# All eight PSUM banks by a table, a leftover load moved to GpSimd, a split last block and a new searched order for a fused linear-attention and MoE kernel

## Chip, cores and metric

One core of one Trainium2 chip. The metric is device time in microseconds (us) for one execution. Most executions of the kernel before agree within about 0.3%. The TensorE clock that the throttle granted is listed for each run as a mean share (1.0 is full clock).

## The reference, cut to what matters

```python
# q, k, v: (8 batches, 8 heads, 576, 64); omega: (128, 64)
def phi(x):                                   # random features, x already scaled
    h = x @ omega.T - (x*x).sum(-1, keepdims=True) / 2
    return exp(h - h.max(-1, keepdims=True)) / sqrt(128)
kv  = einsum('bhsm,bhsd->bhmd', phi(k), v);  z = phi(k).sum(axis=2)
att = einsum('bhsm,bhmd->bhsd', phi(q), kv) / (einsum('bhsm,bhm->bhs', phi(q), z)[..., None] + 1e-6)
x   = att.transpose(0, 2, 1, 3).reshape(4608, 512)
h   = x @ w_in                                # 512 -> 2048, "stage 1"
out = (h * sigmoid(1.702 * h)) @ w_out        # 2048 -> 512, "stage 2"
```

The 576 positions of a head are 512 plus a leftover of 64. The leftovers of all heads form their own small tiles (QL, TL, QKL, VPL) and at the end the ninth row block of the MoE part.

## The kernel before

The program first builds a graph of 1533 operations (1540 after the change). Five fixed lists (`ORDER`) say in which order each engine runs its operations, and a table (`BANK`) says which of the eight PSUM banks (H0 H1 O0 O1 P0 P1 S0 S1) each group of matmuls takes. Waits between engines follow from the graph: an operation waits for what it reads, for a buffer to be free, for the user before it of the same group of matmuls in PSUM, and for the last user of its bank.

```python
def schedule(self):
    self.order = {e: [ops[i] for i in ORDER[e]] for e in ENGINES}
    names = iter(BANK)
    for op in ops:
        for gr in op.opens:
            gr.bank = next(names)
    for op in self.order[PE]:                 # a bank is taken over only after its last user
        for gr in op.opens:
            for o in last.get(gr.bank, ()):
                op.deps.setdefault(o.i, False)
...
# leftover q/k of batch b: by GpSimd with a cast (b >= QL_SW = 2), or f32 by SyncE plus a cast instruction
pool = b >= QL_SW
...
# DMA transposes on SyncE: queries/keys of a tile (TT), leftovers (TL), attention output (XT)
g.add(SP, lambda e: e.dma_start_transpose(tout, tin), ...,
      reads=[("q", s, t), ("k", s, t)], writes=[("Tk", tt), ("Tq", tt), ("tgo", b, t)], ...)
g.add(SP, lambda e: e.dma_start_transpose(xo, xi), ...,
      reads=[("o", os_, 0), ("o", os_, 1)], writes=[("xt", t, b), ("xt", t, b + 1)], ...)
...
attend(0)
for b in range(1, B):
    stage1(b - 1)                             # reads ("xt", t, b - 1)
    if b >= 2:
        stage2(b - 2)
    attend(b)
    if b + 1 < B:                             # loads of the next batch, all on GpSimd
        gate = [("wout", 2)] if b == 1 else [("tgo", b, 2)]
        load_qk(b + 1, 0, 4, ..., after=gate); load_qk(b + 1, 4, 4, ..., after=gate)
        load_ql(b + 1, ..., after=gate);       load_v(b + 1, 0, NT, ..., after=gate)
```

The `gate` says what a load has to wait for beside its own buffer: here that tile 2 of batch b has been transposed.

Names in the profiles: HT, OB, PB and SB are the banks H, O, P and S; XT is the transposed attention output OO, TT and TL are the transposed q/k of a tile and of the leftovers (loaded into QK, and into QL, through QLF where a cast follows); VP and VPL are products with v on GpSimd; TH and GT are the gate of the MoE part on ScalarE and VectorE, OS an output block.

Of the kernel before, what the change touches and what calls it, by code (L numbers as in the profile page):

```python
# [7 lines left out]
ALU = mybir.AluOpType  # L8
# [6 lines left out]
PE = "pe"  # L15
# [3 lines left out]
SP = "sp"  # L19
# [10 lines left out]
BANKS = dict(b0="H0 H1 O0 O1 P0 P1 S0 S1", b1="O1 P0 P1 S0 S1", b2="O1 P0 P1 S0 S1", bv="H0 H1 P0 P1 S0 S1", H="H0 H1", O="O0 O1", Oend="O0 O1 P0 P1")  # L30
# [5 lines left out]
QL_SW = 2  # L36
# [13 lines left out]
    om=(30.0, 0.0, 400.0), qk=(45.0, 1200.0, 770.0), ql=(26.5, 600.0, 630.0), qlc=(26.5, 800.0, 770.0), vl=(26.0, 600.0, 640.0),  # L50
    v=(51.0, 1600.0, 700.0), vw=(51.0, 1200.0, 640.0), qkl=(45.0, 1000.0, 770.0), w=(78.0, 2000.0, 810.0), T=(25.3, 100.0, 1250.0), os=(90.0, 100.0, 620.0),
# [6 lines left out]
        88, 50, 10, 54, 52, 66, 57, 56, 90, 71, 65, 72, 93, 99, 92, 115, 120, 98, 119, 142, 78, 144, 147, 117,  # L58
        152, 80, 146, 153, 125, 105, 83, 126, 132, 110, 107, 86, 219, 134, 137, 159, 113, 221, 253, 164, 140,
        161, 251, 223, 217, 167, 231, 172, 277, 169, 255, 175, 275, 301, 299, 178, 241, 303, 246, 184, 243,  # L60
        181, 265, 249, 187, 267, 270, 193, 279, 273, 196, 202, 313, 383, 211, 315, 289, 318, 205, 291, 294,
        190, 389, 297, 214, 199, 390, 208, 321, 391, 338, 335, 392, 347, 356, 384, 341, 395, 396, 353, 344,
        397, 398, 365, 457, 401, 402, 362, 350, 417, 385, 371, 359, 409, 403, 404, 477, 380, 368, 427, 386,
        437, 377, 467, 432, 429, 556, 472, 487, 374, 469, 447, 492, 562, 489, 449, 563, 557, 452, 564, 558,
        559, 565, 610, 574, 575, 576, 577, 650, 514, 582, 511, 568, 508, 520, 630, 569, 529, 517, 570, 590,
        538, 526, 571, 620, 535, 523, 729, 622, 532, 625, 660, 640, 544, 600, 541, 665, 645, 662, 735, 553,
        605, 602, 730, 642, 547, 550, 736, 763, 737, 731, 732, 755, 687, 738, 684, 693, 741, 681, 783, 742,
        773, 743, 775, 702, 778, 696, 744, 803, 747, 748, 749, 750, 823, 690, 813, 705, 793, 818, 815, 699,
        795, 902, 708, 798, 833, 714, 838, 903, 835, 711, 723, 908, 720, 956, 717, 904, 909, 936, 726, 854,
        910, 860, 905, 863, 857, 928, 914, 866, 911, 869, 915, 946, 920, 966, 875, 971, 948, 916, 917, 976,  # L70
        921, 878, 951, 968, 872, 996, 922, 986, 881, 923, 1129, 890, 884, 991, 1075, 1006, 988, 1101, 899,
        1076, 1011, 1109, 893, 1008, 887, 1081, 1082, 896, 1169, 1083, 1077, 1084, 1078, 1093, 1149, 1094,
        1033, 1119, 1095, 1030, 1027, 1124, 1087, 1042, 1088, 1051, 1036, 1121, 1089, 1139, 1045, 1060, 1090,
        1282, 1039, 1096, 1141, 1144, 1048, 1159, 1274, 1054, 1302, 1248, 1057, 1179, 1161, 1063, 1292, 1164,
        1066, 1181, 1184, 1294, 1249, 1072, 1069, 1322, 1260, 1297, 1250, 1261, 1342, 1251, 1203, 1206, 1266,
        1332, 1267, 1352, 1215, 1212, 1334, 1312, 1262, 1337, 1357, 1263, 1224, 1354, 1221, 1254, 1233, 1314,
        1200, 1255, 1317, 1209, 1218, 1256, 1227, 1257, 1236, 1242, 1427, 1245, 1364, 1428, 1373, 1230, 1268,
        1382, 1239, 1429, 1361, 1269, 1370, 1391, 1415, 1379, 1400, 1416, 1388, 1417, 1397, 1406, 1418, 1367,
        1409, 1410, 1487, 1411, 1376, 1481, 1385, 1394, 1412, 1403, 1482, 1421, 1483, 1433, 1436, 1422, 1442,
        1484, 1445, 1423, 1454, 1451, 1424, 1460, 1488, 1489, 1463, 1439, 1490, 1448, 1430, 1457, 1512, 1505,  # L80
        1466, 1499, 1500, 1501, 1469, 1502, 1526, 1478, 1527, 1506, 1493, 1507, 1475, 1513, 1472, 1494, 1495,
        1514, 1508, 1515, 1496, 1519, 1520, 1521, 1522, 1528, 1529,
    ],
    ACT: [
        51, 89, 9, 60, 61, 59, 70, 73, 75, 74, 101, 68, 102, 95, 100, 97, 122, 124, 129, 154, 151, 156, 127,
        155, 128, 133, 149, 220, 87, 160, 114, 141, 226, 218, 225, 236, 237, 235, 227, 173, 238, 233, 170, 260,
        261, 257, 176, 259, 179, 242, 262, 308, 309, 185, 305, 182, 266, 250, 307, 188, 310, 194, 285, 284,
        197, 286, 203, 283, 281, 212, 206, 191, 215, 200, 209, 339, 336, 393, 348, 357, 342, 345, 354, 399,
        366, 463, 459, 461, 462, 363, 351, 422, 464, 419, 423, 421, 360, 424, 412, 413, 411, 372, 405, 482,
        483, 381, 481, 484, 369, 479, 387, 442, 443, 441, 439, 444, 378, 375, 560, 616, 615, 566, 617, 612,  # L90
        614, 578, 655, 656, 652, 515, 512, 584, 585, 654, 509, 521, 586, 636, 657, 632, 530, 635, 518, 595,
        634, 539, 597, 527, 637, 592, 572, 536, 524, 596, 594, 533, 545, 542, 554, 548, 551, 768, 769, 765,
        733, 688, 770, 759, 757, 685, 758, 767, 739, 694, 788, 682, 787, 789, 790, 703, 785, 697, 808, 745,
        805, 809, 807, 810, 751, 829, 828, 691, 825, 827, 706, 830, 700, 709, 715, 712, 724, 721, 961, 958,
        962, 960, 718, 941, 727, 963, 938, 943, 855, 861, 940, 942, 906, 864, 858, 932, 930, 912, 931, 870,
        867, 876, 918, 982, 981, 983, 980, 978, 879, 873, 1001, 1002, 998, 1000, 1003, 882, 924, 1135, 1133,
        891, 1134, 1131, 885, 1104, 1103, 1136, 900, 1105, 1115, 1114, 894, 1111, 1113, 888, 897, 1173, 1174,
        1171, 1116, 1085, 1175, 1176, 1155, 1153, 1151, 1034, 1079, 1031, 1028, 1043, 1154, 1156, 1052, 1037,
        1046, 1061, 1091, 1288, 1287, 1040, 1284, 1097, 1286, 1049, 1277, 1278, 1289, 1055, 1308, 1276, 1304,
        1058, 1307, 1306, 1064, 1067, 1073, 1070, 1328, 1327, 1326, 1324, 1309, 1348, 1252, 1329, 1344, 1347,  # L100
        1349, 1204, 1346, 1207, 1216, 1213, 1264, 1225, 1222, 1234, 1201, 1210, 1219, 1228, 1258, 1237, 1243,
        1246, 1365, 1374, 1231, 1383, 1240, 1362, 1270, 1371, 1392, 1380, 1401, 1389, 1398, 1419, 1407, 1368,
        1377, 1386, 1395, 1413, 1404, 1434, 1437, 1443, 1485, 1446, 1455, 1452, 1425, 1461, 1464, 1440, 1491,
        1431, 1449, 1458, 1467, 1470, 1479, 1503, 1476, 1473, 1509, 1516, 1497, 1523, 1530,
    ],
    DVE: [
        4, 5, 8, 19, 14, 2, 11, 3, 12, 6, 55, 53, 58, 69, 91, 13, 67, 96, 116, 94, 121, 143, 123, 79, 145, 150,
        118, 148, 81, 106, 84, 85, 82, 108, 111, 109, 112, 138, 135, 139, 136, 222, 254, 165, 162, 163, 252,
        166, 224, 168, 234, 232, 278, 174, 256, 258, 171, 276, 302, 300, 177, 180, 304, 247, 248, 244, 245,
        186, 306, 183, 268, 269, 271, 272, 189, 195, 280, 282, 198, 314, 204, 274, 290, 213, 316, 317, 292,  # L110
        295, 296, 293, 207, 319, 192, 320, 216, 298, 201, 322, 210, 340, 337, 349, 358, 343, 346, 355, 460,
        458, 367, 364, 418, 352, 420, 410, 361, 373, 480, 478, 382, 428, 370, 440, 438, 468, 430, 433, 431,
        473, 474, 488, 434, 448, 470, 493, 471, 490, 450, 451, 376, 379, 453, 491, 454, 494, 613, 611, 651,
        653, 583, 516, 513, 510, 631, 522, 633, 531, 519, 591, 593, 540, 528, 621, 537, 525, 623, 626, 627,
        534, 661, 624, 641, 546, 601, 666, 646, 663, 647, 667, 664, 606, 543, 555, 643, 644, 607, 603, 604,
        552, 764, 549, 756, 766, 689, 686, 695, 786, 774, 683, 776, 784, 779, 777, 780, 704, 804, 698, 806,
        826, 824, 814, 692, 794, 819, 820, 707, 816, 817, 796, 797, 701, 799, 800, 834, 710, 716, 836, 839,
        840, 837, 713, 725, 957, 959, 722, 719, 939, 937, 728, 856, 862, 865, 859, 929, 871, 868, 947, 967,
        949, 972, 950, 973, 877, 979, 977, 952, 953, 969, 970, 874, 997, 999, 987, 880, 883, 1132, 1130, 992,
# [225 lines left out]
def bass_performer_favor__then__act_gelu_quick_kernel(  # L345
# [136 lines left out]

    def load_ql(b, key, ckey, after=()):
        s = b % 2
        pool = b >= QL_SW
        if b in LWB:
            for nm, t, c in (("k", kd, 1), ("q", qd, 0)):
                dst = bass.AP((QL if pool else QLF)[s], 256 * c, [[512, 128], [1, 256]])
# [620 lines left out]
```

## Time and profile before

| | before |
|---|---|
| median of the runs beside the first runs of the change | 324.53 us (324.12 to 325.43, 4 runs) |
| span in the profile | 321.7 us |
| first matmul starts / last matmul ends | 5.67 / 317.71 us |
| first reduction on VectorE (maxima of a projection) | 10.58 us |
| first stage-1 matmul / first GT on VectorE | 26.50 / 28.74 us |
| TensorE time lost in gaps before 40 us / after | 8.3 / 4.7 us |

The gaps are taken from the starts of all matmuls: what each is above the usual distance for its kind. The prediction shows the lines and says how they are read. From 40 us on TensorE is the bound, and it stands still nearly nowhere.

### The profile page before, as it was taken

How to read it: one execution, taken by the hardware profiler on the slowest of the kernel's cores; microseconds unless marked ns; L12 is line 12 of the kernel's file. 1: busy time of each engine (PE TensorE's matmuls, PEld its weight loads, DVE VectorE, ACT ScalarE, POOL GpSimd, SP SyncE). 2: the span in 40 equal slices, each digit the busy share in tenths (PEclk: the TensorE clock that was granted, in tenths of full speed). 3: DMA queues.
4: the chain of work that ended last, by engine and by line, in shares of the span. 5: the costliest groups of instructions: out<-in, count | busy, mean ns of one | idle time of the engine just before them, and what ended most of it. 6: DMA issues, size and time to landing. Idle time of an engine off the chain costs nothing.

```text
span 321.7 us, 5787 instructions
## 1 busy us (share of the span) xinstructions
PE 307.4 (96%) x2246; PEld 151.2 (47%) x2246; DVE 190.7 (59%) x401; ACT 187.3 (58%) x378; POOL 113.1 (35%) x185
## 2 busy tenths in 40 slices
PE   1798999999999999999999999999999999999994
PEld 1574554445544544454454544454544444444442
DVE  0899985368656784686648745788574533342210
ACT  1789855489178646665658766686545543343231
POOL 6696283627019705933644364031200000000000
PEclk9999999999999999999999999999999999999999
DMA  7999999996889989998999999933022002011005
GB/s 134 241 226 222 207 210 222 151 145 129 209 163 206 226 120 162 245 193 155 141 159 194 207 158 168 151 99 61 2 41 86 0 2 98 33 67 65 33 17 148
DMA packets 84119, 44.20 MB, mean 137 GB/s; under 512 B 54844, under 2 KB 77756, under 8 KB 84092
## 3 DMA queue, kind: packets, MB, share of 16 engines
q0 software_dynamic: 29792, 20.45, 42.0%
q1 hardware_dynamic: 54300, 23.37, 35.4%
q8 instruction: 18, 0.29, 0.4%
q14 instruction: 9, 0.07, 0.1%
HBM read 36.73 MB, written 9.44 MB: 144 GB/s over the span
## 4 chain that ended last, share of the span: by engine, by line
PE 86%; ACT 5%; DVE 5%; DMA 2%; issue 1%; POOL 1%; POOLq 0%
PE HT L427 36%; PE OB L427 34%; PE PB L427 11%; PE SB L427 4%; ACT QKP L641 3%; DMA QK<-in_q_dram 2%; DVE GT L966 1%; DVE NM L631 1%; ACT TH L961 1%; DVE OO L855 1%; ACT QKL L641 1%; POOL QK L478 1%; DVE TT L598 0%; DVE RD L847 0%; PE PB L868 0%
## 5 line engine op out<-in xcount | busy, mean ns | idle before, releaser
L966 DVE SCALAR_TENSOR_TENSOR GT<-TH,HT 128x512 bf16<-128x512 f32 x144 | 97.8, 683 | 80.4 <-ACT TH L961 80.0
L427 PE MATMUL HT<-XT,WIN 128*128 128x512 bf16 x576 | 142.2, 379 | 0.6 <-DVE GT L966 0.3
L961 ACT ACTIVATE TH<-HT 128x512 f32<-128x512 f32 x144 | 86.2, 600 | 82.7 <-PE HT L427 74.9
L427 PE MATMUL OB<-WOUT,GT 128*128 128x512 bf16 x496 | 122.5, 379 | 0.0
L427 PEld LDWEIGHTS HT<-XT,WIN 128*128 128x128 bf16 x576 | 52.7, 98 | 61.5 <-DVE GT L966 7.7
L427 PEld LDWEIGHTS OB<-WOUT,GT 128*128 128x128 bf16 x496 | 45.7, 98 | 53.4 <-issue 3.4
L780 POOL TENSOR_TENSOR VP<-VS,WW 128x512 bf16<-128x512 f32 x32 | 33.5, 1050 | 38.8 <-ACT WW L774 38.7
L641 ACT ACTIVATE QKP<-PB 128x512 bf16<-128x512 f32 x54 | 31.4, 600 | 7.2 <-PE PB L427 4.1
L641 ACT ACTIVATE QKP<-SB 128x512 bf16<-128x512 f32 x56 | 33.0, 606 | 2.8 <-PE SB L427 1.1
L995 ACT ACTIVATE OS<-OB 128x512 f32<-128x512 f32 x31 | 18.6, 599 | 16.7 <-PE OB L427 16.6
L631 DVE TENSOR_REDUCE NM<-SB 128x4 f32<-128x512 f32 x31 | 20.9, 682 | 8.8 <-PE PB L427 7.4
L631 DVE TENSOR_REDUCE NM<-PB 128x4 f32<-128x512 f32 x23 | 15.5, 683 | 6.9 <-PE PB L427 5.3
L427 PE MATMUL PB<-WOUT,GT 128*128 128x512 bf16 x80 | 19.4, 379 | 0.0
L478 POOL DMA_DIRECT2D QK<-in_k_dram x17 | 13.4, 790 | 7.1 <-DMA QK<-in_q_dram 4.2
L789 POOL CAST VP<-WW 128x8 bf16<-128x8 f32 x32 | 7.0, 225 | 24.3 <-ACT WW L774 24.3
L855 DVE TENSOR_TENSOR OO<-PB,RD 128x320 bf16<-128x320 f32 x29 | 13.7, 485 | 0.4
L478 POOL DMA_DIRECT2D QK<-in_q_dram x17 | 13.0, 768 | 0.0
L503 POOL DMA_DIRECT2D QL<-in_k_dram x12 | 7.8, 649 | 13.6 <-DMA TT<-QK 13.6
L427 PEld LDWEIGHTS PB<-WOUT,GT 128*128 128x128 bf16 x80 | 7.8, 98 | 9.5 <-DVE GT L966 0.3
L855 DVE TENSOR_TENSOR OO<-SB,RD 128x320 bf16<-128x320 f32 x24 | 11.5, 482 | 0.3
L532 POOL DMA_DIRECT2D VS<-in_v_dram x12 | 7.8, 661 | 7.2 <-DMA TT<-QK 7.2
L427 PE MATMUL PB<-TT,omB 64*128 64x512 bf16 (+1 forms) x31 | 10.2, 377 | 0.0
(140 smaller groups left out, 285.7 us busy)
## 6 DMA issues: line engine op xcount, KB each, us to landing
out_dram<-OS SPq DMA_DIRECT2D x32, 256.0 KB, 2.8
VS<-in_v_dram POOLq DMA_DIRECT2D x12, 512.0 KB, 6.6
QK<-in_k_dram POOLq DMA_DIRECT2D x15, 256.0 KB, 6.4
QK<-in_q_dram POOLq DMA_DIRECT2D x15, 256.0 KB, 7.3
WIN<-in_moe_w_in_dram POOLq DMA_DIRECT2D x4, 512.0 KB, 10.7
WOUT<-in_moe_w_out_dram POOLq DMA_DIRECT2D x4, 512.0 KB, 17.2
VS<-in_v_dram SPq DMA_DIRECT2D x4, 256.0 KB, 6.4
VS<-in_v_dram SPq DMA_DIRECT2D x2, 512.0 KB, 12.4
```

The lines of the kernel that those rows point to most:

```text
L427: return lambda e: e.matmul(o() if callable(o) else o, lhsT=l, rhs=r, **kw)
L478: POOL, lambda e, dst=dst, so=so: e.dma_start(dst, so), 800, key,
L503: POOL if pool else SP, lambda e, dst=dst, so=so: e.dma_start(dst, so), 120, key,
L532: SP if b < V_SW else POOL, lambda e, dst=dst, so=so: e.dma_start(dst, so), 120, key,
L631: lambda e: e.tensor_reduce(out=o, in_=bass.AP(TILE[gr.bank], 0, [[512, 128], [128, 4], [1, 128]]), axis=AX.X, op=ALU.max, negate=True,),
L641: lambda e: e.activation(out=o, in_=view(gr, 0, pat or [[1, 512]])(), func=ACTF.Exp, scale=scale),
L780: lambda e: e.tensor_tensor(out=VP[vs][:, :, 0:64], in0=bass.AP(V, t * 9 * 64 + 64, [[NT * 9 * 64, 128], [64, 8], [1, 64]]), in1=bass.AP(W ...
L789: POOL, lambda e: e.tensor_copy(out=VP[vs][:, :, 64], in_=WW[vs][:, :]), 140, key + K_W + 240,
L855: lambda e, gr=gr, x=x: e.tensor_tensor(out=OO[os_][:, 5 * x : 5 * x + 5, :], in0=bass.AP(TILE[gr.bank], 0, [[512, 128], [65, 5], [1, 64]] ...
L961: lambda e, gr=gr, th=th: e.activation(out=TH[th][:, :], in_=at(gr, 0, 512)(), func=ACTF.Tanh, scale=0.851),
L966: lambda e, gr=gr, th=th, jc=jc: e.scalar_tensor_tensor(out=GT[gi][:, jc, :], in0=TH[th][:, :], scalar=1.0, in1=at(gr, 0, 512)(), op0=ALU. ...
L995: lambda e, gr=gr, os_=os_: e.activation(out=OS[os_][:, :], in_=at(gr, 0, 512)(), func=ACTF.Copy, scale=0.5),
```

## The change

Its intent: more banks for stage 1, so that TensorE can run further ahead of its readers; one cast and two SyncE issues fewer at the start; a shorter way out after the last matmul; and a new order of all five engines, found by a search over five scenarios of late loads and of the clock's phase. Cut to its core:

```diff
-QL_SW = 2
+QL_SP = (1,)          # only batch 1's leftover q/k go by SyncE with a cast; batch 0's go by GpSimd
+TAIL = True
 ORDER = {             # new lists for PE, ACT, DVE, POOL and SP (1540 numbers)
-        88, 50, 10, 54, 52, 66, 57, 56, 90, 71, ...
+        49, 10, 65, 87, 64, 91, 89, 114, 141, 51, ...
 BANK = """            # before: stage 1 only on H0 and H1; after: all groups over all eight
-S0 S1 O0 P0 O1 S0 O1 P1 H0 P0 P0 H0 O0 H1 O1 ...
+S0 H0 P1 P1 S1 P1 S0 S1 S1 H1 P1 P0 P1 P1 O0 ...
-        pool = b >= QL_SW
+        pool = b not in QL_SP
+    def last_block(gi, key):      # the last 128x512 output block in two halves of 256 columns
+        for half in range(2):
+            ...                   # 16 matmuls of 256 columns each
+            cut = 128 if half else 256
+            ...                   # ACT copies columns 0:cut; for the second half DVE copies 128:256
+            for h in range(2):
+                g.add(ACT if half and h else SP, ...)    # the very last store is issued by ScalarE
```

Also changed: the pools in `BANKS` (the table decides, they feed nothing), constants of the search's cost model, and a branch for split leftovers that no batch reaches.

## The prediction

> **What bounds the kernel now.** I read the page's slices first, then the busy time by stage, then the chain of waits in order of time, then the timelines of the start and of the end.
>
> The slices (40 of 8 us; a digit is a tenth of busy time):
>
> ```profile
> PE   1798999999999999999999999999999999999994
> DVE  0899985368656784686648745788574533342210
> ACT  1789855489178646665658766686545543343231
> POOL 6696283627019705933644364031200000000000
> ```
>
> TensorE is short of work in the first three or four slices and in the last one, and nowhere else. The table by stage says it in microseconds:
>
> ```profile
> 0.00:40.00 40.00, 30.39 (x355) 19.54 (x356) 29.44 (x77) 29.06 (x65) 25.82 (x45) 1.00 1.16 206
> 40.00:240.00 200.00, 199.31 (x1534) 96.92 (x1533) 133.88 (x285) 127.16 (x261) 87.31 (x140) 1.00 0.95 157
> 240.00:318.00 78.00, 77.71 (x360) 34.75 (x358) 27.34 (x41) 30.76 (x53) 0.00 (x0) 1.00 0.16 53
> 318.00:321.70 3.70, 0.00 (x0) 0.00 (x0) 0.00 (x0) 0.34 (x1) 0.00 (x0) 1.00 0.57 127
> ```
>
> (Columns after the length: PE, PEld, DVE, ACT, POOL, clock, DMA share, GB/s.) "Busy" of TensorE flatters it, since matmul ends are modelled. So I also took the starts of all 2246 matmuls from the trace and added up what each gap is above its usual length (216 ns for a 128x512 matmul, 310 for a pair of 64-row ones, 56 or 32 for the small ones). The sum is 13.0 us: 8.3 us before 40 us, 4.7 us after. Of the 4.7 us about 3.5 us is one pattern: some 35 gaps of 311 or 312 ns instead of 216, each where a 128-row matmul is followed by the first 64-row projection of the attention. A new order does not remove those. With the first matmul at 5.67 us and 4.0 us from the last matmul's end (317.7) to the end of the span, the account is 5.7 + 8.3 + 4.7 + 4.0 = 22.7 us without work on TensorE and 299.0 us of matmul stream. Only the 22.7 can shrink.
>
> Why the start is slow, from the chain of waits in order of time (start us, length us):
>
> ```profile
> 1.24 1.61 POOL QK L478 x2
> 2.85 6.19 DMA QK<-in_q_dram
> ...
> 13.25 1.46 ACT QKP L641 x3
> ...
> 26.66 1.47 ACT QKP L641 x3
> ...
> 28.21 0.50 ACT TH L961
> 28.71 0.02 issue
> 28.73 0.69 DVE GT L966
> 29.42 1.20 DVE NM L631 x2
> 30.62 0.60 DVE GT L966
> ```
>
> Loads hold it up to about 9 us. From about 11 us to 40 us ScalarE and VectorE alternate on the chain: both are nearly full, and TensorE waits for them. From 40 us on the chain is TensorE. So what counts at the start is **when VectorE and ScalarE begin their real work**, since they then run without a pause. VectorE begins late:
>
> ```profile
> DVE om_raw L449 <- DMA om_f<-in_omega_dram: 6.6, 1, 6.6
> ```
>
> That small load of omega is the fourth issue on SyncE, behind the three leftover loads. The first big reduction on VectorE (NML) starts only at 10.58 us, the first for a main tile at 11.19 us.
>
> The end, from the timeline:
>
> ```profile
> 316.64 2.83 SPq L1012 DMA_DIRECT2D out_dram<-OS  x4
> 317.75 0.60 ACT L995 ACTIVATE OS<-PB 128x512 f32<-128x512 f32 x1 [1.13 <-PE PB L427]
> ```
>
> After the last matmul: a copy of 0.60 us, two stores issued one after the other on SyncE (0.58 us each), then 2.4 us from issue to landing.
>
> **What the Trainium skill says.** "TensorE: Matmul & The Clock Gate", Back-to-back issue gap: N / 2.4 + 2.5 ns when warm. The trace agrees: four 512-column matmuls take 0.86 us, 216 ns each. By the same formula 256 columns cost 109 ns (estimate), so halving a block costs almost nothing. "Perfetto Trace Analysis", Matmul Optimizations, asks that all 8 PSUM banks be used. The kernel uses all 8 already, but MoE groups of stage 1 rotate over two. The wait list of TensorE after 40 us has a single entry, 0.6 us, so this trace shows little that more banks could give. "DMA: Bandwidth & Descriptors", Issuing engines are not separate DMA queues: all transfers share the same 16 engines, and moving an issue saves only sequencer time. The trace fits: the engines carry 1.2 to 1.4 transfers at once from 3 us on, so every load moved out of the first microseconds lets the others land earlier. The same page, SWDGE vs HWDGE vs iDMA: a cast during the transfer needs GpSimd. This is what allows the cast on VectorE to go.
>
> **The change, part by part.**
> 1. Bank table. The table alone gives the banks; the changed BANKS line feeds nothing in emission. The 144 groups of stage 1 now use all eight. From the two orders with the durations above, the median TensorE work between a bank's last use and its next opening by a stage-1 group goes from 2.3 to 3.4 us, but 20 groups instead of 1 have under 1.6 us. Avoidable gaps after 40 us: 4.7 - 3.5 = 1.2 us. I expect **0.7 us** of them to go.
> 2. Batch 0's leftover q/k by SWDGE. Goes: one 0.42 us cast on VectorE and two SyncE issues (0.81 and 0.62 us) at the very start. Comes: two issues of about 0.76 us on GpSimd, which was idle for 4.2 us from 6.7 us on, waiting for q.
> 3. The new order at the start. SyncE issues one v load, then omega, then a load that must wait for q of the second tile; the other v loads thus stay out of the way. GpSimd issues k, k, q, k and a leftover before building the identity. Working it: GpSimd starts at 1.24, five issues of 0.76 end at 5.04, the identity (0.29, its memset now on VectorE) is there at about 5.5. So the first transposes start at 5.6 us, no earlier than now. Omega is issued at about 1.4 instead of 2.91; with the same 4.6 us to landing it is there by 6.0 (estimate, rather less with less traffic), cast to 6.2, transposed to 6.5, copied to 7.0. The first K projection follows, 0.43 us, and the first reduction on VectorE starts at about 7.6 instead of 10.58: 3.0 us of lead. But VectorE had already done two copies of 0.42 us that now come later, so 2.1 us, plus the 0.42 us of the cast: 2.5 us at most. The two engines' lists up to the first stage-1 result are about as long as before (22.3 against 23.4 us of durations on VectorE, 24.1 against 21.3 on ScalarE with two or three instructions of batch 1 moved ahead). ScalarE's sixth instruction needs q of the first tile, now issued sixth, landing near 10 us: some of the lead is lost there. I take **2.2 us**.
> 4. The last block in two halves of 256 columns. 32 x 109 = 3.49 instead of 16 x 216 = 3.46 us: nothing lost. At the end 128 columns are copied on ScalarE beside 128 on VectorE, about 0.26 instead of 0.60 us; the last two stores are issued in parallel on SyncE and ScalarE, which saves one 0.58 us issue. Together **0.9 us**.
> 5. The new branch for split leftovers needs a batch that is both at least RT (1) and in LWB (0): it never runs. The descriptor counts and cost constants only served the search.
>
> Sum: 0.7 + 2.2 + 0.9 = 3.8 us; 324.75 - 3.8 = 320.95, say **320.9 us**.
>
> **The rivals.**
> (a) The lead at the start is eaten. GpSimd has vector-product work behind four more issues that wait for q and for ScalarE, and v now lands later. If the first V products wait for v or GpSimd, VectorE and ScalarE run dry once and the gain is only the tail and a little: about 323. For it: GpSimd is 60 to 90% busy in those slices. Against it: the first V product is at 15.85 us now, and the new list gives about 16.2 with the reductions ahead of it as filler.
> (b) The start gains more, because loads without competition land in about 3 us instead of 4.4 to 7 and free banks let TensorE run ahead between 29 and 40 us (there the gaps sum to about 1.6 us). Then 4 us at the start, 1 in the middle, 1 at the end: about 318.5. For it: in the chain the bank waits of stage 1 on GT stand at 30.62 and later. Against it: these waits are mostly VectorE's own load, which more banks don't lighten.
> (c) The order was found on a model and meets lateness on the chip: new waits in the middle cost what the rest gains, 324 to 325. Against it: TensorE has 66 to 70% busy helpers there and the search covered late loads.
>
> **Range and chances.** Rivals (a) to (b) span 318 to 324; I put 8 of 10 on 318.0 to 323.6. Over 2% faster means under 318.3: it needs 6.5 us of the 19.2 us that are not structural, more than every part at its best guess: 0.12. Slower than 331.2 would need a new stall in the TensorE-bound stretch: 0.01. Within 2%: 0.87.
>
> **What would show it.** Right: first transposes near 5.6 us but the first main reduction near 7.6; the first stage-1 GT about 2 us before 28.7; TensorE's gaps after 40 us down from 4.7 to about 4 us, the 311 ns gaps still there; 3.1 us from last matmul to end. Wrong: an idle stretch of VectorE or ScalarE over 1 us between 8 and 28 us (rival a), or single TensorE waits over 0.5 us after 40 us (rival c), or TensorE gaps before 40 us down by 4 us or more (rival b).

## The result, and the profile after

Ratios here are the mean of one kernel's fast runs over the mean of the other's fast runs of the same rounds, so not quite the ratio of the medians quoted.

| | before | after |
|---|---|---|
| median | 324.53 us (324.12 to 325.43) | 329.17 us (327.62 to 330.11) |
| ratio | | 1.0135 [1.0086, 1.0183] |
| granted clock of the runs | 1.0 in the profile | 0.990, 0.995, 0.990, 0.995 |
| span in the profile | 321.7 | 328.3 |
| first matmul / last matmul ends | 5.67 / 317.71 | 5.49 / 325.01 |
| first main reduction / first stage-1 matmul / first GT | 11.19 / 26.50 / 28.74 | 7.59 / 30.62 / 32.85 |
| from the last matmul's end to the end | 4.0 | 3.3 |

It is 1.35% slower, where 1.2% faster was predicted. The slices of the page after:

```profile
PE   2889999999999997999869999999999999999995
DVE  1767985567946773577635865687666334333220
ACT  2877972489386554665753678573843435333331
POOL 7567445095179233716048217211120000000000
PEclk9987999999999999999999999999999999999999
```

Two things are new. TensorE has holes in the middle (the 16th slice, and the 20th and 21st), where it had none. And the clock falls at the start (the third and fourth slices). The table by stage from 120 to 170 us, first before, then after (length, then PE, PEld, DVE, ACT, POOL, clock, DMA share, GB/s):

```profile
120.00:170.00 50.00, 50.00 (x369) 23.80 (x368) 31.81 (x65) 31.77 (x67) 26.24 (x42) 1.00 1.08 173
```

```profile
120.00:170.00 50.00, 43.65 (x312) 20.68 (x317) 28.27 (x57) 30.69 (x65) 20.87 (x34) 1.00 1.09 178
```

This stretch of 50 us loses 6.35 us of TensorE. The stretches beside it lose little: from 40 to 120 us TensorE goes from 79.89 to 79.16 us, from 170 to 240 us from 69.42 to 69.26. The waits of TensorE from 100 to 240 us, after (engine, line, waited for: us in total, times, longest):

```profile
PE PB L428 <- issue: 2.6, 1, 2.6
PE HT L428 <- issue: 2.3, 2, 2.2
PE PB L428 <- DMA XT<-OO: 1.0, 1, 1.0
```

Before, the same list has one entry of 0.6 us. "Issue" means that the profile found no releaser here; the chain of waits names it. Two stretches of that chain after (start us, us, what):

```profile
117.88 8.18 DMA XT<-OO
126.06 1.83 issue
127.89 1.02 PE HT L428 x4
...
151.21 9.35 DMA XT<-OO
...
160.61 1.04 PE PB L428 x4
```

XT<-OO is the DMA transpose of the attention output, which stage 1 of that batch needs. It takes 8 to 9 us to land here. This is the view of DMA issues from 110 to 170 us, before and then after (the last number is the median us from issue to landing):

```profile
XT<-OO SPq DMA_TRANSPOSE x8, 2.7
TL<-QL SPq DMA_TRANSPOSE x2, 2.5
```

```profile
XT<-OO SPq DMA_TRANSPOSE x8, 7.0
TL<-QL SPq DMA_TRANSPOSE x2, 8.2
```

And the timelines of SyncE's queue and of GpSimd at this place say what else was under way. Before:

```profile
114.78 4.44 SPq L878 DMA_TRANSPOSE XT<-OO  x3
...
124.26 0.81 POOL L478 DMA_DIRECT2D QK<-in_k_dram  x1 [0.21 <-issue]
```

After:

```profile
116.63 3.96 SPq L906 DMA_TRANSPOSE XT<-OO  x3
...
117.78 0.79 POOL L479 DMA_DIRECT2D QK<-in_k_dram  x1 [9.34 <-DMA TT<-QK]
...
119.30 0.77 POOL L479 DMA_DIRECT2D QK<-in_q_dram  x1
```

Before, the next batch's loads start 5 us after the last of the three transposes was issued. After, GpSimd has them earlier in its list, and big loads of k, v and q go out while the transposes are still being issued (SyncE is busy with the three until 120.6 us). The same happens around 148 us. The median of 7.0 us is the worst of the three profiles of the change: the two taken later have 5.1 us (after_again) and 4.7 us (after_third) for XT here, and TensorE is busy for 45.59 and 48.28 of these 50 us. That was the first theory for the middle: the loads crowd the transposes.

### The profile page after: what moved, and what is told of

It is laid out like the page before. It is cut to its first block, busy times and chain, and to the rows that moved or that the text cites.

```text
span 328.3 us, 5783 instructions
## 1 busy us (share of the span) xinstructions
PE 306.7 (93%) x2224; PEld 155.5 (47%) x2262; DVE 189.3 (58%) x400; ACT 185.6 (57%) x382; POOL 113.9 (35%) x185
## 4 chain that ended last, share of the span: by engine, by line
PE 83%; DMA 9%; DVE 2%; issue 2%; SPq 1%; ACT 1%; POOL 0%; POOLq 0%
PE OB L428 27%; PE HT L428 21%; PE SB L428 18%; PE PB L428 16%; DMA XT<-OO 5%; DMA QLF<-in_q_dram 2%; DMA QK<-in_q_dram 1%; DVE OO L883 1%; SPq L504 1%; SPq L545 1%; POOL QK L479 0%; DVE GT L994 0%; PE PB L896 0%; ACT TH L989 0%; DVE RD L875 0%
## 5 line engine op out<-in xcount | busy, mean ns | idle before, releaser
L428 PE MATMUL OB<-WOUT,GT 128*128 128x512 bf16 x308 | 77.2, 379 | 0.9 <-issue 0.5
L994 DVE SCALAR_TENSOR_TENSOR GT<-TH,HT 128x512 bf16<-128x512 f32 x49 | 33.4, 683 | 33.7 <-ACT TH L989 33.5
L428 PE MATMUL HT<-XT,WIN 128*128 128x512 bf16 x190 | 48.8, 379 | 2.7 <-issue 2.5
L428 PEld LDWEIGHTS OB<-WOUT,GT 128*128 128x128 bf16 x320 | 29.2, 98 | 34.0 <-issue 2.4
L989 ACT ACTIVATE TH<-HT 128x512 f32<-128x512 f32 x49 | 29.5, 605 | 26.4 <-PE HT L428 22.2
L428 PE MATMUL SB<-XT,WIN 128*128 128x512 bf16 x141 | 36.3, 379 | 0.1
L994 DVE SCALAR_TENSOR_TENSOR GT<-TH,SB 128x512 bf16<-128x512 f32 x36 | 24.3, 681 | 17.4 <-ACT TH L989 17.1
L428 PE MATMUL PB<-XT,WIN 128*128 128x512 bf16 x122 | 31.6, 379 | 2.1 <-DMA XT<-OO 1.0
L428 PEld LDWEIGHTS HT<-XT,WIN 128*128 128x128 bf16 x196 | 18.0, 98 | 22.9 <-issue 3.7
L428 PE MATMUL OB<-XT,WIN 128*128 128x512 bf16 x104 | 26.7, 379 | 0.2
L428 PE MATMUL HT<-WOUT,GT 128*128 128x512 bf16 (+1 forms) x110 | 25.1, 364 | 0.1
L428 PE MATMUL SB<-WOUT,GT 128*128 128x512 bf16 (+1 forms) x95 | 21.6, 361 | 0.1
L428 PEld LDWEIGHTS SB<-XT,WIN 128*128 128x128 bf16 x144 | 13.5, 98 | 15.2 <-DVE OO L883 0.3
```

What stands on the lines that cost most here:

```text
L428: return lambda e: e.matmul(o() if callable(o) else o, lhsT=l, rhs=r, **kw)
L989: lambda e, gr=gr, th=th: e.activation(out=TH[th][:, :], in_=at(gr, 0, 512)(), func=ACTF.Tanh, scale=0.851),
L994: lambda e, gr=gr, th=th, jc=jc: e.scalar_tensor_tensor(out=GT[gi][:, jc, :], in0=TH[th][:, :], scalar=1.0, in1=at(gr, 0, 512)(), op0=ALU. ...
```

## Experiments

Each ratio is to the kernel before in the same set of runs, on the same chip: chip 10 for start_before, start_after, tail_only and banks_age; chip 7 for swdge_only, after_spfirst, after_warm and after_gate; chip 6 for after_again, after_pool, after_sp, after_lightload, after_gate2, best1 and best2; chip 9 for after_third and gate2_again. A run over 1.5% above the fastest of its kernel counts as slow and is left out of the ratio; medians and ranges are of all runs. An order spliced from both kernels keeps for each group of matmuls the bank that it had where its order comes from.

### The parts alone

**start_before**: the changed kernel with the start of the kernel before (all that its first 77 operations of TensorE need).

```diff
 ORDER: start (first 77 PE operations and what they need): after -> before; rest as after
-QL_SP = (1,)
+QL_SP = (0, 1)
```

> The first 285 operations (up to the first stage-2 group, about 40 us) in the order, banks and queues of the kernel before; the rest and the tail as in the kernel after. Theory: the changed kernel loses about 3 to 4 us at the start (late leftover load of batch 1, then half clock) and about 5 us in the middle, and gains 0.7 us at the end. So this one keeps the middle loss and has no start loss: granted clock 1.00, first stage-1 matmul at about 26.5 us, total 325 to 327. Rival (all of the loss is at the start): 320 to 323. Rival (all of it is in the middle order): 328 to 330.

Measured: 326.26 us (322.81 to 329.77), before 324.79, ratio 1.0008 [0.9961, 1.0056]; the run of 329.77 us is left out as slow. Even with the old start, and at full clock, TensorE waits 2.0 us until 126.4 us and twice 0.55 us around 160, and is busy for 46.41 of the 50 us from 120 us on. So the new middle (its order and its banks) is bad of itself. One expectation failed: the first stage-1 matmul came at 28.30 and not at 26.5 us. The same start in tail_only has it at 27.49 us, so single profiles of one start differ by 1 us or more.

**start_after**: the start of the change (its first 255 operations), the rest as before, no split tail.

```diff
 ORDER: start as after; rest: after -> before
-TAIL = True
+TAIL = False
```

> The complement: the first 255 operations as in the kernel after (leftovers of batch 0 by GpSimd, its orders), the rest and the tail as in the kernel before. Theory: start loss of 3 to 4 us alone, clock 0.99 or 0.995, total 327 to 329; no wait of TensorE over 1 us after 60 us. Rival (the loss is in the middle): 324 to 325.

Measured: 323.47 us, 0.9971 [0.9941, 1.0000], no wait over 1.1 us after 60 us. My theory that the start alone lost 3 to 4 us falls: on its own it gains about 0.9 us (0 to 1.9).

**tail_only**: the kernel before with the split last block.

```diff
-TAIL = False
+TAIL = True
```

> The kernel before with only the last block in two halves. From the last matmul's end to the end of the span 3.98 us before and 3.26 us after: expect 0.6 to 0.9 us faster than before. Rival (stores landing set the end anyway): within 0.2 us of before.

Measured: 323.54 us in 5 rounds, 0.9961 [0.9940, 0.9981]: 1.3 us gained (0.6 to 1.9). The end of the timeline of the changed kernel shows the mechanism (the last store issued by ScalarE):

```profile
325.04 0.28 ACT L1022 ACTIVATE OS<-SB 128x128 f32<-128x128 f32 x1 [1.36 <-PE SB L428]
325.35 0.29 DVE L1030 TENSOR_SCALAR OS<-SB 128x128 f32<-128x128 f32 x1 [10.67 <-ACT OS L1022]
325.68 0.64 ACTq L1040 DMA_DIRECT2D out_dram<-OS  x1
```

The two copies do not run side by side, as they were meant to: VectorE starts 0.03 us after ScalarE has ended, and the two take 0.60 us, as long as the one copy before. The graph orders the users of one group of matmuls one behind the other, and both copies read the same group. In all profiles with the split block that were looked at it is so; what is gained is gained at the stores.

**banks_age**: the order of the kernel before, and a table over all eight banks that gives each group the bank that has been free longest.

```diff
 BANK: -stage 1 on H0, H1      +every group: the bank free longest, of all eight
```

> The kernel before with its orders and queues untouched, but every PSUM group put on the bank that has been free longest, over all eight. Theory: TensorE hardly waits for banks after 40 us, so within 0.7 us of before, if anything faster between 29 and 40 us. Rival (two banks hold stage 1 back): 1.5 us faster or more.

Measured: 323.13 us in 5 rounds, 0.9960 [0.9929, 0.9992]: 1.3 us gained (0.3 to 2.3). I had given 0.7 us to the table, which this doesn't exclude. It is not the table of the change, which was not run with the old order.

**swdge_only**: the kernel before, with batch 0's leftover q/k issued by GpSimd as its third and fourth loads and the cast on VectorE gone.

```diff
-QL_SP = (0, 1)
+QL_SP = (1,)
 ORDER[POOL]: + the two leftover loads in places 3 and 4;  ORDER[DVE]: - the cast
```

> The kernel before with only the leftovers of batch 0 issued by GpSimd with the cast in the transfer (third and fourth in its list), without the cast on VectorE. Theory: the identity and the q loads are issued 1.4 us later, VectorE saves 0.42 us: between 0.5 us faster and 1.5 us slower than before. Rival (the cast during the transfer is what makes the changed kernel slow): 3 us slower or more.

Measured: 323.72 us, 0.9962 [0.9919, 1.0004]: about 1 us, not proven.

So each part that was tried alone is good or harmless. What loses is the new middle.

### Mending the changed kernel, and misses

**after_spfirst**: only the first ten issues on SyncE reordered, so that batch 1's leftover comes earlier.

```diff
 ORDER[SP]: behind omega first v and leftover v of batch 0, then batch 1's four leftover loads in one go
```

> The kernel after with only the head of SyncE's list changed: the loads that wait for nothing (v and leftover v of batch 0) first, then the four leftover pieces of batch 1 in one go. Theory (late leftover pieces start the loss): the last of the four is issued at about 10.4 instead of 12.7 us and lands near 16 instead of 20.0, no wait of 1.2 us at 19.3, clock 1.00; 2.5 to 4 us faster than the kernel after. Rival (early v loads crowd out q and k): first reduction on VectorE 1 us later and no gain, 328 to 330.

Measured: 326.66 us (324.44 to 329.40), 1.0028 [0.9955, 1.0102]. Its profile is of the run of 329.40 us, which counts as slow, so it carries little. In it the last leftover piece was issued by 11.3 us and VectorE no longer waited for it, yet the cast came at 21.39 us, not earlier than the 20.00 us of the change: VectorE was late, with its first main reduction at 8.47 instead of 7.59 us. This is the sign that the rival had named. The mechanism that I expected didn't show, so the better time says nothing about it.

**after_warm**: twelve small matmuls put into TensorE's wait at the start, to keep its clock up.

```diff
+g.warm = {220: [mm(at(wop.grps[0], 0, 256), ident[:], omB[:]) for _ in range(12)]}
```

> The kernel after, with 12 dummy matmuls of 256 columns (1.3 us) put into TensorE's wait for the leftover transposes of batch 1 at 19.3 us; same data path, same lateness. Theory (the wait lets the clock fall to half for two windows of 3.41 us, and the slow attention matmuls are then the chain): clock back to 1.00, 2 to 3 us faster than the kernel after, first stage-1 matmul at 27 to 28.5 us. Rival (the load's lateness itself costs, the clock is only a symptom): within 0.7 us of the kernel after, first stage-1 matmul still near 30.6 us.

Measured: 329.73 us, 1.0161 [1.0112, 1.0210], no gain (the change itself was not run in this set). The half clock at the start was gone from the profile, but another such window came at 159.7 us, behind a wait of 3.5 us for XT. So the slow clock at the start isn't the main loss.

**after_gate**: all loads from batch 3 on wait also for the XT transposes of the batch two before theirs. Six loads of the last batch had to move behind two products of GpSimd for that.

```diff
-gate = [("wout", 2)] if b == 1 else [("tgo", b, 2)]
+gate = [("wout", 2)] if b == 1 else [("tgo", b, 2)] + [("xt", t, b - 1) for t in range(NT)]
```

> The kernel after with the loads of the next batch made to wait, on GpSimd, until the output transposes of the batch before the current one have landed (and six loads of the last batch moved behind two products so that this can't lock up). Theory (early loads crowd the DMA transposes): the transposes land in about 3 us instead of 8 to 9, the waits of TensorE of 2.3 us at 125 us and of 1.1 and 2.8 us near 160 us go, 3 to 5 us faster than the kernel after. Rival (SyncE's own order, stores ahead of transposes, makes them late): the transposes still land late, within 1 us of the kernel after, or slower where the loads then come late.

Measured: 328.03 us, 1.0099 [1.0056, 1.0143]. The waits at 125 and 160 us are gone, but a new one came. TensorE's longest wait from 170 to 240 us, and the entry in GpSimd's timeline that explains it:

```profile
PE OB L412 <- POOL VPL L706: 3.7, 1, 3.7
```

```profile
187.58 0.65 POOL L517 DMA_DIRECT2D VS<-in_v_dram  x1 [11.31 <-DMA XT<-OO]
```

A held-back load blocks GpSimd for 11.3 us, and the products behind it in its list come too late. (Line numbers differ from the changed kernel's because the lists are printed in fewer lines; L412 is its L428.)

**after_again**: the changed kernel once more, on another chip.

```diff
 (no edit)
```

> The kernel after once more, for a second profile. The six profiles so far show a long wait of TensorE for transposes in the middle in every kernel with the middle order of after, but at other places, and the half clock in other windows. Theory (the middle order stalls TensorE wherever transposes land late, and any stall of 2 us or more can halve the clock for a window of 3.4 us): 327 to 331 again, long waits between 120 and 200 us again, the wait at 19 us and its half clock perhaps not. Rival (the wait at 19 us is a fixed loss): it is there again with 1.3 us.

Measured: 326.13 us (324.38 to 327.01), 1.0058 [1.0022, 1.0095]. Its profile ran at full clock and waits 2.1 and 1.8 us in the middle. The loss is there without the slow clock, but smaller. The expectation that any stall of 2 us or more can halve the clock found no support: no half clock followed the wait of 2.1 us. By the profile this wait is one for ScalarE, 6 us after the one for XT; with the gate it is gone too (gate2_again).

**after_pool** and **after_sp**: GpSimd's loads, or all of SyncE's list after the start, in the order of the kernel before, the rest as changed.

```diff
 after_pool: ORDER[POOL]: loads after the start in the places that they had before
 after_sp:   ORDER[SP]:   after the start as before
```

> The kernel after with one list changed: from 40 us on, GpSimd's loads stand at the slots where they stand in the kernel before, its products in the order of after between them. Theory (loads issued some 6 us earlier crowd the DMA transposes): transposes in the middle land in about 3 us, waits at 125 and 160 us gone or under 1 us, 2.5 to 5 us faster than after. Rival (SyncE's order): no gain, within 1 us of after.

> The kernel after with one other list changed: from 40 us on SyncE issues its transposes and stores in the order of the kernel before. Rival theory (stores and later transposes ahead in the in-order queue make the awaited transposes late): 2.5 to 5 us faster than after. Theory (crowding by the loads): issue order of SyncE matters little, within 1.2 us of after, transposes still landing in 7 us or more.

Measured: 333.29 us, 1.0287 [1.0231, 1.0342], and 351.93 us, 1.0876 [1.0807, 1.0944]. Both far worse: the first waits 4.1 us for TL and several times for GpSimd's products, the second 6.1 us for TT and 5.5 us for TL. XT landed in 3.1 and 2.7 us in the median from 110 to 170 us; for after_sp I had expected 7 us or more and a time near that of the change, and was wrong on both. The five lists fit each other, and one engine's old list is no remedy. This could not separate the causes.

### The disputed cost by itself

**after_lightload**: the changed kernel, same instructions and same waits, but the main q, k and v loads of batches 3 to 7 move a quarter of their bytes. The result is wrong (relative error 0.91).

```diff
-[[H * 512, 128], [512, nh], [1, 256]]
+[[H * 512, 128], [512, nh if b < 3 else 1], [1, 256]]      # the same for v
```

> Wrong result on purpose: the kernel after with every list as it is, but each q, k and v load of batches 3 to 7 moves only one quarter of its rows. Same instructions, same waits, less traffic. Theory (crowding): transposes land in under 3.5 us, no wait of TensorE over 1 us between 100 and 210 us, clock 1.00, 321 to 324.5. Rival (order of issue): the waits stay, 326 or more.

Measured: 321.22 us, 0.9917 [0.9896, 0.9937], about 5 us under the changed kernel on the same chip. The stretch that had lost 6.35 us of TensorE is nearly full again:

```profile
120.00:170.00 50.00, 49.42 (x363) 24.09 (x366) 30.74 (x62) 32.65 (x69) 25.26 (x44) 1.00 0.72 129
```

Orders, banks and waits are those of the change. A rival that blamed the order of issues or the bank table as such would have left the waits there. It is the bytes of the loads. Which loads, and whether it isn't their own earlier landing that helps, this run can't tell, since all from batch 3 on were shrunk. XT landed in 3.9 us in the median from 110 to 170 us, not under 3.5 as expected, and TensorE didn't wait for it.

**after_gate2**: the full-size loads again; only those of batches 5 and 6 wait for the XT transposes of the batch two before theirs (the text says "the batch before them", loosely). No list is changed.

```diff
-gate = [("wout", 2)] if b == 1 else [("tgo", b, 2)]
+gate = [("wout", 2)] if b == 1 else [("tgo", b, 2)] + ([("xt", t, b - 1) for t in range(NT)] if b in (4, 5) else [])
```

> The changed kernel; only the loads of batches 5 and 6 wait for the transposes of the batch before them, those of batch 7 (whose gate blocked GpSimd for 11.3 us in after_gate) are as in the change. If the crowding of the DMA transposes by loads issued early is what the middle loses (theory): the waits near 125 and 155 to 165 us go, as in after_gate, no wait over 1 us near 196, and the time is 322 to 324 us, ratio 0.993 to 0.999. If holding loads back always costs as much as it gives, because GpSimd stands still and its products come late (rival): a wait of 2 us or more shows up somewhere after 130 us, and the time stays at 326 or above.

Measured: 320.59 us (320.39 to 321.14), 0.9897 [0.9880, 0.9913]. This is under the expected range, at the predicted time, and it beats the kernel before by 1%. The change itself had 326.13 us on this chip in an earlier set (after_again), where the kernel before had 324.21 us as against 324.20 here: 5.2 us between the means.

**after_third** and **gate2_again**: the change and after_gate2 unchanged, on one chip, since the change had not been run in one set with after_gate2.

```diff
 (no edit)
```

> The changed kernel as it is, on the same chip as gate2_again. It had 329.17 us on one chip and 326.13 us on another. If crowding by the loads of batches 5 and 6 is what costs (theory): 325 to 330 us here too, 1.5 to 2.5% above gate2_again, with waits of TensorE over 1 us between 120 and 170 us. If the gain of after_gate2 came from its chip and not from the gate (rival): within 0.5% of gate2_again.

> after_gate2 once more, unchanged. Theory: 320 to 321.5 us, ratio to before 0.988 to 0.992, no wait of TensorE over 1 us between 120 and 170 us. Rival (the earlier chip flattered it): 323 us or more.

Measured: after_third 325.84 us, six runs from 321.92 to 329.62; gate2_again 321.66 us, six runs from 321.24 to 324.21, ratio to before 0.9942 [0.9907, 0.9976]. The ratio given for after_third, 0.9998 [0.9953, 1.0043], leaves out its two runs over 329 us as slow. Fast runs alone have means of 324.31 and 322.31 us, 2.0 us or 0.6% apart, which with four and six runs of this spread is not clear of noise and less than the 1.5 to 2.5% that I expected. The clocks of the two slow runs are 0.990 and 0.995, as in the four runs of the result; with them the mean is 326.03 us and the difference 3.7 us. So the gate's gain over the change is clear in time on chip 6; on chip 9 it is clear in the profiles only. The size of the loss itself didn't repeat: over the three sets the ratio of the change to the kernel before is 1.0135, 1.0058 and, without its slow runs, 0.9998. The median of gate2_again is 0.16 us above what I expected, because two of its runs had a clock of 0.989; the ratio is above the expected range for the same reason. Nothing is left of the waits: the list of TensorE's waits from 100 to 240 us is empty in gate2_again. Its stage, its landings from 110 to 170 us, and the order of issues:

```profile
120.00:170.00 50.00, 50.00 (x370) 24.08 (x369) 30.26 (x62) 33.12 (x70) 29.93 (x48) 1.00 1.10 188
```

```profile
XT<-OO SPq DMA_TRANSPOSE x7, 2.6
TL<-QL SPq DMA_TRANSPOSE x3, 3.3
```

```profile
114.09 3.84 SPq L890 DMA_TRANSPOSE XT<-OO  x3
...
120.08 0.79 POOL L463 DMA_DIRECT2D QK<-in_k_dram  x1 [14.18 <-DMA XT<-OO]
```

The first load now waits for the transposes and starts 2.2 us after the last of them was issued. Without the gate it starts 1.2 us after the first of the three began. The best comparison is with after_again, whose profile also ran at full clock and whose transposes are issued at the same time:

```profile
114.14 3.84 SPq L906 DMA_TRANSPOSE XT<-OO  x3
...
116.95 0.79 POOL L479 DMA_DIRECT2D QK<-in_k_dram  x1 [11.00 <-DMA TT<-QK]
```

So the transposes need not be late for the collision (the kernel before issues them at 114.78 us): here only the loads differ, by 3 us, and the landings of XT are 5.1 against 2.6 us. It repeats at 145 us (145.00 and 144.96 us for the transposes, 143.19 and 149.43 us for the first load). The engines move no fewer bytes in the stretch (188 GB/s against 178 in the result, 189 in after_again): the fix costs no throughput, it only puts the short transfer that TensorE waits for ahead of the long ones that nobody waits for yet.

### Do the parts add?

**best1**: the order of the kernel before with the leftover by GpSimd, the split tail and the banks by age. **best2**: the start of the change, the rest as before, with split tail and banks by age.

```diff
 best1: ORDER as before;  QL_SP = (1,);  TAIL = True;  BANK by age
 best2: ORDER: start as after, rest as before;  TAIL = True;  BANK by age
```

> The orders of the kernel before with three parts of the change that were each good alone: leftover of batch 0 by GpSimd (0.9962), last block split (0.9961), all eight banks by age (0.996). If the parts add, 0.988, 320.9 us; since the first and third both work on the start and banks, I expect 0.989 to 0.993, 321 to 322.5 us. If their gains are the same microseconds counted twice: 0.995, 323.2.

> The start of the changed kernel (its first 255 operations), then the order of the kernel before, the last block split, all eight banks by age: start 0.9971, tail 0.9961, banks 0.996, product 0.989, 321.3 us; 320.5 to 322.5 if they add. Without a wait over 1.2 us after 60 us. If the start's gain depends on the bank table it was found with: about 323.

Measured: best1 322.53 us, 0.9950 [0.9930, 0.9969]; best2 325.49 us, 1.0021 [0.9991, 1.0051]. They don't add, as far as the intervals tell. best1 keeps less than half of the product of the three ratios (0.9883, or 3.8 us); best2 keeps nothing, with two of six runs at a clock of 0.989 and a wait of 1.1 us until 42.2 us. Gains of some 1 us in a kernel with fitted lists can't simply be summed. The version that beats both is after_gate2.

## Why the prediction was wrong, point by point

**The step that failed is rival (c), and what I wrote against it.** I gave it 324 to 325 us and set it aside with "TensorE has 66 to 70% busy helpers there and the search covered late loads". The share of busy time was also read a little too high (the table of the prediction gives 67% for VectorE and 64% for ScalarE). Both statements missed what matters. The sign named for (c), single waits over 0.5 us after 40 us, came: 2.6, 2.2 and 1.0 us. Helpers aren't short of time; the transfers that carry their results to TensorE are. And that the search had tried late loads doesn't mean that the lists are safe on the chip. SyncE's XT transposes wait for the attention results; GpSimd's loads wait only for an older transpose, and the new list has them some 7 us earlier (117 to 118 instead of 124 us), at the time of the transposes. Shown: the landings go from 2.7 to 7.0 us (5.1 and 4.7 in the two other profiles), quarter-size loads take the waits away (after_lightload), and so does making two batches' loads wait for the transposes, with all bytes and lists kept (after_gate2, gate2_again). In the result the transposes came another 2.5 us later than in after_again (116.63 and 114.14 us), after half clock at the start; that this lateness made its loss larger is argued only. Why the search didn't see the collision stays open.

**Part 1, "0.7 us of 1.2 us".** The account of gaps after 40 us was right for the kernel before, but I used it as if the new order could only shorten it. In the profile of the result the middle lost 6.35 us instead. Banks by age alone gave 1.3 us (0.3 to 2.3), so the runs don't show the term itself to be too large.

**Part 3, "I take 2.2 us".** The first main reduction came at 7.59 us, as worked out (7.6). But the lead didn't reach stage 1: the first GT came at 32.85 us and not 2 us before 28.7. The chain at the start of the changed kernel:

```profile
12.72 7.25 DMA QLF<-in_q_dram
...
20.00 0.48 DVE QL L510
```

The leftover load of batch 1, for which the cast stays on VectorE, is issued late on SyncE (behind loads that wait for q of the second tile) and lands at 19.98 us. VectorE stands still 1.7 us for it, and TensorE 1.2 us. I had worked through when VectorE begins, not through which later load it would meet. In the other profiles this wait is shorter (0.8 us in after_again), and there the first GT comes at 29.4 to 32.3 us, still later than before's 28.74 (though the old start, too, has it later in other profiles: 29.50 us in tail_only, 30.31 us in start_before). The start on its own was worth 0.9 us (start_after, 0 to 1.9), not 2.2. A reading was too high as well: the DMA engines carry 1.2 to 1.4 transfers at once only from 8 us on (1.16 to 1.45, by the microsecond); from 3 to 8 us it is 0.86 to 1.18.

**A loss that I hadn't named: the clock.** At the start, the changed kernel got half the clock for 6.8 us:

```profile
22.00:28.00 6.00, 6.00 (x76) 5.08 (x74) 4.21 (x13) 3.07 (x8) 4.20 (x8) 0.50 1.27 227
```

Over three sets of runs, 10 of 14 executions of the changed kernel had a mean clock of 0.995 or less, and 2 of 11 of the gated one. The average of the changed kernel's four others is 324.4 us, that of the gated kernel's nine others 321.1 us. So at full clock some 3.3 us are lost, by the profiles to the waits. In gate2_again two runs with a clock of 0.989 took 323.92 us on average and the four others 321.51, 2.4 us less. But in after_again the run with 0.989 was the fastest of four (324.38 us), so what the half clock costs isn't settled. Where in a run the windows fell is only known for profiled runs. Why the same start meets them in some runs and not in others stays open.

**Part 2** was right in kind: about 1 us at best for the leftover by GpSimd, within noise. **Part 4**, 0.9 us: 0.7 us in the profile of the change, 0.5 in that of tail_only, 1.3 us (0.6 to 1.9) in the timed tail_only. The number fits, but half of the mechanism failed: the copy of "0.26 instead of 0.60 us" took 0.60 us, one half after the other. That the sum still fits is luck. **Part 5**: the branch is dead, as said.

**The sum.** 3.8 us were expected; with the crowding taken away 3.3 us arrive in after_gate2 (1.03% of 324.2 us) and 1.9 us in gate2_again (0.58%, two of its six runs at a clock of 0.989). That this comes near is partly luck in the terms: the start gave less, the tail by another way. **Rivals (a) and (b)**: what (a) describes, VectorE dry for over 1 us between 8 and 28 us, did happen, through the QL load and not through the V product. (b) did not: the profile's first stage-1 matmul came later, not earlier.

**The chances.** The class was right, 329.17 us is 1.35% over. The range was far too narrow above: I had allowed a new wait in the middle to cost only as much as the rest gained.

## What to carry to other kernels

When two engines issue DMAs from fixed lists, an order that a search found on a model need not hold on the chip; where a short transfer has the bound engine waiting, put a dependence between it and the bulk loads rather than trust in the order, and put it only where the collision is, since a held-back issue blocks everything behind it on its engine. Before calling the middle of a kernel safe, list the transfers that the bound engine waits for, see how long they take to land, and ask which loads the change brings beside them. To find a suspected crowding, shrink the loads and keep every instruction: it separates bytes from order in one run; a gate that only delays them then shows which loads it is.

## What the Trainium skill lacked or had wrong

- "DMA: Bandwidth & Descriptors", Issuing engines are not separate DMA queues, is right: a transpose on SyncE landed after 2.7 us in the median in the kernel before, after 4.7 to 7.0 us in the change, where GpSimd issued loads during it, and after 2.6 us with the gate. I found no page that gives a landing time of an SBUF-to-SBUF DMA transpose under load, or that says to make bulk loads wait for such a transfer.
- "TensorE: Matmul & The Clock Gate", the table of goals, asks to avoid idle gaps over about 3 us in the middle of a kernel. Here half clock came for 6.8 us from 21.5 us on in a profile (after_third) in which, after the first matmul, no wait of TensorE before it was longer than 0.7 us; the 3.4 us before it had 2.53 us of busy TensorE. No busy share to go by comes out of this: gate2_again had 2.55 us in a stretch of the same length (14.7 to 18.1 us) and kept full clock. (Elsewhere the same page does allow for frequent short idles; it gives no figure by which to tell the two apart.)
- "Perfetto Trace Analysis", Matmul Optimizations, asks for all eight banks, but not how to tell what they are worth. The kernel before had no wait on a bank over 0.6 us after 40 us, and banks_age still gained 1.3 us (0.3 to 2.3); where it gained them no run shows.
- No page that I read says that lists for the engines of a kernel that are found together can't be exchanged one by one: after_sp, with one engine's old list, took 8.8% longer than the kernel before.
